# Linear attention with a gated state, then an MLP: one score pair of chunk 3 beside the running sums, and another order of turns

## The chip, the cores and the metric

One core of a Trainium2 chip runs the whole program. The time is device microseconds of one execution; the kernel before has a median of 424.98 us over three runs (424.64 to 425.36). Five engines work beside each other, each in its own program order: TensorE (PE), VectorE (DVE), ScalarE (ACT), GpSimd (POOL), and SyncE (SP), which here only issues DMAs. Semaphores tie them together.

## The reference, cut to what matters

```python
B, H, S, D = 4, 8, 768, 48
for t in range(S):                       # state: [B, H, D, D]
    state = alpha[:, :, t, :, None] * state + einsum('bhd,bhe->bhde', k[:, :, t], v[:, :, t])
    y[:, :, t] = einsum('bhd,bhde->bhe', q[:, :, t], state)
x = y.transpose(0, 2, 1, 3).reshape(B, S, H * D)          # DM = 384
xn = (x - mean) / sqrt(var + 1e-6) * g_ln
out = x + maximum(xn @ w_ch1, 0) @ w_ch2                  # 384 -> 1536 -> 384
```

## The kernel before, in words

The 768 tokens are cut into six chunks (c = 0 to 5) of 128 tokens, and each chunk has four batches b. `attention(c, b)` is one generator for one chunk of one batch; there are 24, named by the letters a to x in the order of `c * 4 + b`, so chunk 3 is m, n, o, p. In a chunk the logarithms of alpha are summed over the tokens by a product with a triangle of ones (the *running sums*, tile `lps`, L310, L313 or L400); from chunk 1 on the sums run over the two halves of 64 tokens apart. ScalarE takes the exponentials (L317, L318), VectorE scales k and q with them (L320, L322, tile `qk`), and both are transposed so that the head dimension lies across partitions: in chunks 0 and 1 by TensorE (L348), from chunk 2 on by VectorE in blocks of 32 x 32 (L359, tile `tr`) and two rounds of DMAs through DRAM: four writes per attention (L365, `td<-tr`) and four reads (L372, into `kT` and `qT`). `tr` lies in a ring of seven buffers (tag `in`) that also holds the raw alpha, k and q.

Then TensorE makes the scores of the four head pairs, 64 x 64 each (L398, tile `aps`); VectorE copies their lower triangle into `at` (L410); the update of the state goes through `ups` (L426), VectorE (L439, tiles `mid` and `st`) and a product with the decay on GpSimd (L441). The outputs `yps` are sums of a product with the state (L457) and one with `at` (L461). ScalarE and VectorE copy them into `x` (L484 and L487), which is also sent to DRAM (L496), normalised, and transposed into `xT` by L520 and L522 or, from chunk 4 on, by L526 and DMAs.

The constant SPLIT decides how the scores of head pair 3 are placed. In a chunk from SPLIT on, they are written into the free columns of the bank that holds the running sums of the attention two further on, with output halves swapped against the other pairs, and their order is alternated with that of pair 2:

```python
split = c >= SPLIT
...
for p, s in () if whole else SCORES if split else np.ndindex(NP, 2):
    for i in range(2):
        rs = slice(64 * i, 64 * i + D)
        to = aps[1][halves[i], 0, s] if split and p == NP - 1 else aps[0][halves[1 - i], p, s]
        nc.tensor.matmul(to, kT[rs, p, s], qT[rs, p, s], start=True, stop=True)
    if ahead:
        ahead.pop(0)()                   # one half of the running sums, two attentions ahead
```

Such a chunk then needs two copies of the triangle (L410, 128 x 384 and 128 x 128) instead of one, two ScalarE copies into `x` (L472, L474) instead of one (L484), two VectorE steps (L477, L480) instead of one (L487), and its swapped half of v is loaded in three DMAs instead of two (L153).

The MLP of chunk 0 is plain: the letters Y and Z make its first product (L556, ReLU in L559), P and Q the second (L568). Chunks 1 to 5 use products of combined blocks, fewer than the plain ones: the letters 1 and 2 make the first products (L846, 15 to a chunk and half, each with its additions on VectorE, L856 to L889, and on GpSimd, L865 to L885), R and U the ReLU (L896), M the second product (L672, additions L682 to L730, L688 on GpSimd). VectorE makes the combined blocks: S and W those of the weights (L798, L632), X those of x (L823), N those of the hidden layer (L659). The letters A to L load the weights as 64-bit floats and turn them into 32-bit floats on VectorE (L215 to L232) and ScalarE (L223). O fetches `kept` copies of x for the sum at the end (L543), and results leave by L547.

All of this is woven together by a literal string, ORDER, with 1508 letters: each letter runs its generator to the next `yield`. The order of each engine's instructions, SyncE's DMAs included, is the order in which these turns issue them; no scheduler moves anything afterwards.

Of the kernel before, what the change touches and what calls it, by code (L numbers as in the profile page):

```python
# [19 lines left out]
STAGED = 3  # L20
BY_DMA = 2
X_BY_DMA = 4
SPLIT = 4
AHEAD = 2
G = 32
SCORES = ((0, 0), (0, 1), (1, 0), (1, 1), (3, 0), (2, 0), (3, 1), (2, 1))
# [4 lines left out]


ORDER = (
    "aaabacdccbbbacbacbadbabbaadababacccbfbeacaAcCdcdacbfdefffeeddedebdaaccaAacacbaab"
    "ffaefeedddefgbCbbcfbhBgcedfcheaggccbcgahhccghdedddgdbidffdhcAcbhfgedfgghAhidjghi"
    "dehCBBZjfigYZYYZZBkYABZjYiCZZhCZffjliijejDYiZeDZjZYDgghfYeZfheekEEgYjgiZYhYZZYZD"
    "legjeEYFYhhfiZiGFhZkGFfgZEZYigikgfjGlYFejfgYHYfkZlkZlfZYfejZHehjYSleiHjGlnfjIjlY"
    "SjHkmInYggmJIYgPSQhJikYQJlPISgKPQgKSliSehSggnKQkhlhelLnSOhLhnkliLOmmmkPkmmhWWOmO"
    "hPPnWSQSohmWXQXlnXoQpPWXpnSlXlPXkQijSjXmXoj21SOjiWookn2o1Xi2om2kS2mXo1k211Wk2222"
    "2S11nmkSnjlimpnplj2ppijJpkrp1m1SW211m1lji1m21212m1linmlnWinURk22pW2q1lr1k2O2jqji"  # L40
    "12i1mn1o1nplnXmUp2pkrrRkrolp1rr2qpU2q11pkRW2Mr2qoM1Uqnk2qlopnMp1RoppoMU1oNLlWNMW"
    "NOosqsRNMNrpm2MNoqtMkkt2lMNM11MonmMrqrqpqtRoXUqMNspttM2MqtNtMsNMNnqNsMMOMtMsMXvX"
    "MMNMMstNsNXqMMOvMnMMrmNXmMuMqMnMnrtruoqpXtrMosX1orMrMvM21q12Xvts1Ot2sr1rMutvXXqu"
    "12211p12u122ru21t1u1222v1O221p221m1Ru2m2U2X22UnqO1v11sxt1w12w2n21usts2Rutpuwsu1K"
    "wU1R2M12vw1qURw1M2NU1or2RMMNMvtMsxtNwooNMsMMM1supvMuvwRNuNwsrUxNNMsMxMNoMrNNMMNt"
    "xMtMMvxxNqMMoMNXMMMMMXMtqMMNqXwvuMMNvxtrMMwXXMM1xMX2OM1tqX1wvstX122221X11rM2u2xu"
    "x1xxwvq221tw2s21xu1w2Xs2ssv1111x2uu1122v22OX212xw11v2r12sUxOR12121wRsUUR112r1xu2"
    "Ux22wNxMsuRU121NRr2N1vMvNNNNMwNMMMMwMNtOuNMXMUMMqXMXMxRXMMNMNwMuvMMMxNM1xMMMXMNN"
    "MXMMNMvMM2MXMXvwuMMMMMXw2X1xw21X1xw2221x11111111112212222OR12O1v222121vwR12U2M2O"
    "2221121211UUR1XR1M222MR11R2XX2XXUM1X2XXOMMNNMN1NUM1XM121NNNNMMU111122M1MN111M1N2"  # L50
    "1MN21MXR2MM21112121X211M1M1MMN1R22M2N2MM22MMRMMO11NM1N2MM1R22UUM2NMMM222222MUMMN"
    "2RMM2MMO2MUNNRUMNNMMOOMMNMMMNNNMMMNMMUMMMNMMMNNMNMMMMMNMMMNMMMMMMMMM"
)


# [1 line left out]
def kernel(  # L57
# [68 lines left out]
    def load(c, m, names):  # L126
# [12 lines left out]
        if "v" in names:  # L139
# [4 lines left out]
            if c:  # L144
# [4 lines left out]
                parts = ((0, 0, NP, NP), (1, 0, NP, 0))  # L149
                if c >= SPLIT:  # L150
                    parts = ((0, 0, NP, NP - 1), (1, 0, NP - 1, 0), (1, NP - 1, 1, H - 1))
# [139 lines left out]
    def attention(c, b):  # L291


        whole, last = c == 0, c + 1 == NCB
        split = c >= SPLIT
        if whole and b % 2 == 0:
# [661 lines left out]
```

## Time and profile before

| what | value |
|---|---|
| median of three runs | 424.98 us |
| the profiled execution, its own time | 425.54 us |
| its span, first to last instruction | 423.8 us |
| mean granted TensorE clock | 0.996 |
| busy: PE, DVE, ACT, POOL | 413.1, 353.8, 179.0, 151.8 us |
| DMA issues by SyncE | 397 |
| DMA, mean | 145 GB/s; 0.9 and more of the 16 engines' time until 90 us, 0.11 in the last 64 us |

The profiled execution took 1.74 us more than its span, and 0.56 us more than the median. A busy engine in this table is one with an instruction in it; the idle time of an engine matters only where the last chain of work runs through it.

### The profile page before, as it was taken

The page shows a single profiled execution, that of the slowest core. Times are in us where ns is not written, and L with a number is a line of the kernel's source. Part 1 is how long each engine was busy: PE and PEld are TensorE (multiplying, and loading weights), DVE is VectorE, ACT ScalarE, POOL GpSimd, SP SyncE. Part 2 cuts the span into 40 slices and gives each one's busy share as a digit, 9 for nine tenths or more (in the row PEclk, how much of TensorE's full clock was granted, in tenths as well). Part 3 has the DMA queues.
Part 4 walks back from the last instruction along what each step waited for, and adds up shares of the span by engine and source line. Part 5 has one row for each costly group of instructions (what it writes and reads, how often), then busy time and mean ns, then how long its engine had stood idle before and what let it go on. Part 6 is the DMA issues. An engine that isn't in the chain of part 4 may idle for free.

```text
span 423.8 us, 11541 instructions
## 1 busy us (share of the span) xinstructions
PE 413.1 (97%) x4608; PEld 364.3 (86%) x4608; DVE 353.8 (83%) x711; ACT 179.0 (42%) x440; POOL 151.8 (36%) x164
## 2 busy tenths in 40 slices
PE   8999999999997999999999999999999999999997
PEld 6887888756686888998888999889998899999996
DVE  3999999999997899895989996679966789757873
ACT  5696447635044566443336612535512333112200
POOL 1010110100022883034395033296051961467314
PEclk9999999999999899999999999999999999999999
DMA  8899989797978678795573345516116200001201
GB/s 279 255 340 265 301 187 296 183 267 184 221 202 176 170 171 177 199 215 132 157 116 115 69 121 129 105 38 180 21 57 140 85 0 2 0 19 39 94 20 56
DMA packets 135037, 61.26 MB, mean 145 GB/s; under 512 B 90908, under 2 KB 131100, under 8 KB 134984
## 3 DMA queue, kind: packets, MB, share of 16 engines
q1 hardware_dynamic: 134440, 60.37, 55.2%
q8 instruction: 36, 0.59, 0.6%
q10 hardware_dynamic: 544, 0.17, 0.2%
q14 instruction: 17, 0.14, 0.1%
HBM read 43.12 MB, written 17.39 MB: 143 GB/s over the span
## 4 chain that ended last, share of the span: by engine, by line
PE 70%; DVE 15%; DMA 8%; issue 3%; SPq 2%; ACT 1%; DVEq 0%; ACTq 0%
PE ops L672 28%; PE hps L846 28%; DMA rq<-in_q_dram 3%; PE hps L556 3%; DVE ws L225 2%; DMA td<-tr 2%; PE aps L398 2%; PE yps L457 2%; DVE w L217 2%; PE yps L461 2%; PE ups L426 1%; DVE tr L359 1%; SPq L365 1%; DVE w L229 1%; DMA gate<-row 1%
## 5 line engine op out<-in xcount | busy, mean ns | idle before, releaser
L688 POOL TENSOR_TENSOR ob<-ob,u 128x192 f32<-128x192 f32 x40 | 28.6, 726 | 57.4 <-DVE ob L685 43.3
L846 PE MATMUL hps<-sum,w 128*128 128x256 f32 x192 | 46.6, 382 | 0.0
L441 POOL TENSOR_TENSOR mid<-mid,gate 112x192 f32<-112x192 f32 x20 | 12.5, 626 | 87.3 <-DVE mid L439 61.9
L896 ACT ACTIVATE hT<-hT 128x512 f32<-128x512 f32 x48 | 28.7, 625 | 32.0 <-POOL hT L868 12.5
L672 PE MATMUL ops<-w,hT 128*128 128x192 f32 x224 | 40.7, 327 | 0.0
L846 PEld LDWEIGHTS hps<-sum,w 128*128 128x128 f32 x192 | 35.8, 190 | 4.9
L672 PEld LDWEIGHTS ops<-w,hT 128*128 128x128 f32 x224 | 37.1, 190 | 0.9 <-ACT hT L896 0.4
L846 PE MATMUL hps<-xT,w 128*128 128x256 f32 x136 | 35.5, 395 | 0.6 <-DVE st L439 0.6
L556 PE MATMUL hps<-xT,w 128*128 128x256 f32 x144 | 32.7, 383 | 0.1
L568 PE MATMUL ops<-w,hT 128*128 128x384 f32 x96 | 31.7, 487 | 0.0
L556 PEld LDWEIGHTS hps<-xT,w 128*128 128x128 f32 x144 | 26.9, 190 | 4.3 <-DVE mid L439 0.5
L846 PEld LDWEIGHTS hps<-xT,w 128*128 128x128 f32 x136 | 26.4, 198 | 4.3 <-DVE st L439 1.0
L672 PE MATMUL ops<-ws,sum 128*128 128x192 f32 x160 | 28.8, 326 | 0.0
L568 PEld LDWEIGHTS ops<-w,hT 128*128 128x128 f32 x96 | 18.0, 190 | 11.8
L672 PEld LDWEIGHTS ops<-ws,sum 128*128 128x128 f32 x160 | 26.6, 190 | 0.2
L682 DVE TENSOR_TENSOR ob<-ops,ob 128x192 f32<-128x192 f32 x50 | 17.3, 350 | 8.5 <-PE ops L672 6.1
L672 PE MATMUL ops<-ws,hT 128*128 128x192 f32 x128 | 23.6, 328 | 0.7 <-DVE hT L887 0.6
L441 POOL TENSOR_TENSOR st<-st,gate 112x192 f32<-112x192 f32 x16 | 9.9, 625 | 37.0 <-DVE st L439 37.0
L398 PEld LDWEIGHTS aps<-qT,kT 48*64 48x64 f32 x576 | 19.4, 134 | 3.9 <-issue 1.4
L672 PEld LDWEIGHTS ops<-ws,hT 128*128 128x128 f32 x128 | 21.3, 190 | 1.8 <-DVE hT L887 1.0
L398 PE MATMUL aps<-qT,kT 48*64 48x64 f32 x576 | 22.4, 222 | 0.2 <-ACT kT L353 0.2
L461 PE MATMUL yps<-vn,at 64*64 64x48 f32 x320 | 22.6, 220 | 0.0
(247 smaller groups left out, 1134.1 us busy)
## 6 DMA issues: line engine op xcount, KB each, us to landing
ws<-in_moe_w_ch_dram SPq DMA_DIRECT2D x12, 768.0 KB
td<-tr SPq DMA_DIRECT2D x64, 96.0 KB
vn<-in_v_dram SPq DMA_DIRECT2D x12, 384.0 KB
kept<-x SPq DMA_DIRECT2D x24, 192.0 KB
ob<-kept SPq DMA_DIRECT2D x24, 192.0 KB
out_dram<-ob SPq DMA_DIRECT2D x19, 192.0 KB
ra<-in_alpha_dram SPq DMA_DIRECT2D x16, 192.0 KB
kT<-td SPq DMA_DIRECT2D x32, 96.0 KB
```

The source lines that it names most:

```text
L217: stt(out=dst, in0=lo.bitcast(UINT32), scalar=2.0 ** -32, in1=dst.bitcast(INT32), op0=AOP.mult, op1=AOP.add)
L225: stt(out=hi, in0=hi, scalar=-(1 << 31), in1=lo, op0=AOP.bitwise_and, op1=AOP.bitwise_or)
L398: nc.tensor.matmul(to, kT[rs, p, s], qT[rs, p, s], start=True, stop=True)
L441: nc.gpsimd.tensor_mul(new, new, by)
L461: nc.tensor.matmul(yps[r][halves[s], i, p], at[halves[r], p, s], by, start=r != i, stop=True)
L556: nc.tensor.matmul(hps, w1[:, j // 2, f, j % 2 * P:][:, :P], xT_of[0][:, f, bs], start=(f == 0), stop=(f == NF - 1))
L568: nc.tensor.matmul(ops_of[b], hT_of[c][:, j, b], w2[:, j], start=(j == 0), stop=(j == NJ - 1))
L672: nc.tensor.matmul(acc, lhs[:, j], rhs[:, j], start=(j == 0), stop=(j == NT - 1))
L682: nc.vector.tensor_add(x, acc, x)
L688: getattr(nc.gpsimd, f"tensor_{op}")(x, x, y)
L846: nc.tensor.matmul(acc[:, i], w, b, start=True, stop=True)
L896: nc.scalar.activation(out=x, in_=x, func=AFT.Relu)
```

## The change

SPLIT goes from 4 to 3: chunk 3 is now treated as chunks 4 and 5 are. For each of m, n, o and p this means one more VectorE copy (L410), one ScalarE copy more, one VectorE step more, and the swapped placing and order of the scores. There are two more DMAs in all (one for each pair of batches of chunk 3): 399. The number of matmuls stays at 2360.

ORDER is another string: the same letters in the same numbers, drawn differently from its first characters on. So nearly every engine's instructions stand in another order.

```diff
-SPLIT = 4
+SPLIT = 3
...
 ORDER = (
-    "aaabacdccbbbacbacbadbabbaadababacccbfbeacaAcCdcdacbfdefffeeddedebdaaccaAacacbaab"
+    "acaaababccdabacbbcadabdacababbeabcbaacccbbcAabddceaafedfceebafdedaedafeccaedegcA"
...
-    "NOosqsRNMNrpm2MNoqtMkkt2lMNM11MonmMrqrqpqtRoXUqMNspttM2MqtNtMsNMNnqNsMMOMtMsMXvX"
+    "pmNMjjoNNNRnMoo2NproNMOksMMkMNtMMkoMNoNMqmnrsqUkNMqpqqsMnrMtttXWMstNvttNMMnMNXoM"
...
-    "2RMM2MMO2MUNNRUMNNMMOOMMNMMMNNNMMMNMMUMMMNMMMNNMNMMMMMNMMMNMMMMMMMMM"
+    "MNMUM12NMMMMRMN2UNMONMNMNMMMNOMMNMMMNMMURNMNMMMMNMMMMMNNMMMMNMMMMMMM"
 )
```

More of the change, by code (lines that the diff above doesn't have):

```diff
@@ L33 @@
 ORDER = (
-    "aaabacdccbbbacbacbadbabbaadababacccbfbeacaAcCdcdacbfdefffeeddedebdaaccaAacacbaab"
[L35 to L39, printed above, removed]
@@ L40 @@
-    "2S11nmkSnjlimpnplj2ppijJpkrp1m1SW211m1lji1m21212m1linmlnWinURk22pW2q1lr1k2O2jqji"
-    "12i1mn1o1nplnXmUp2pkrrRkrolp1rr2qpU2q11pkRW2Mr2qoM1Uqnk2qlopnMp1RoppoMU1oNLlWNMW"
-    "NOosqsRNMNrpm2MNoqtMkkt2lMNM11MonmMrqrqpqtRoXUqMNspttM2MqtNtMsNMNnqNsMMOMtMsMXvX"
-    "MMNMMstNsNXqMMOvMnMMrmNXmMuMqMnMnrtruoqpXtrMosX1orMrMvM21q12Xvts1Ot2sr1rMutvXXqu"
-    "12211p12u122ru21t1u1222v1O221p221m1Ru2m2U2X22UnqO1v11sxt1w12w2n21usts2Rutpuwsu1K"
-    "wU1R2M12vw1qURw1M2NU1or2RMMNMvtMsxtNwooNMsMMM1supvMuvwRNuNwsrUxNNMsMxMNoMrNNMMNt"
@@ L46 @@
[L46 to L51, printed above, removed]
@@ L52 @@
-    "2RMM2MMO2MUNNRUMNNMMOOMMNMMMNNNMMMNMMUMMMNMMMNNMNMMMMMNMMMNMMMMMMMMM"
+    "acaaababccdabacbbcadabdacababbeabcbaacccbbcAabddceaafedfceebafdedaedafeccaedegcA"
+    "bdeadhdCbcfgabbbfdcdggcfgbfbecffeChBccdfeddcgbfhahhfgddgcahdidhgcbeAjgddfhcAhhfi"
+    "BghiYeAjeYefBZjgCiZYeeZYBYgYjZiCZYjZBZlijZfkiYklYZfDjfgDhDYZhCfZgZifYgjZEEYFEgDe"
+    "YgijYYgGgFgYGYYYEZihjFhkfeZkliiZhYGShGZfZjeHkZgYfZFjhiihjeeeHljlHfYlZheYlfelkkIZ"
+    "iZJPYHIQSJgkPhIZnlQSJISPQjKkSfilgKhmgSgKSfgnPjOnLhlmLlgOnknLhmlmOhhmmlmlQhQOikWj"
@@ new lines @@
+    "PmWWhSnWkQlWmnQnpjPSjSkXXiQoXljPXjXoSniSSX1kmlWipml2m1X1SoXS121XokWo21oi1o1222o2"
+    "mnm1m2inWp2im1qpkp2k1in121Xpknp21lplnji12Sn1Wk2222W2kOpmqmXimjU2j2rUn1iS1R1112o2"
+    "1n2m2nrpOp1pRlP1polrrlokR12nrUMrrWrmqjkppq1l1q12p22lolMtkLR21RpMqNMMqoo1UMOpWqUM"
+    "pmNMjjoNNNRnMoo2NproNMOksMMkMNtMMkoMNoNMqmnrsqUkNMqpqqsMnrMtttXWMstNvttNMMnMNXoM"
+    "sMNsX1Mtnm2MXMMqMMpMNMXXmqMsXMMsoMoqnM1XOqM2o22u212Xrrtqtp1mv1q1sq1oXtrv12O211m1"
+    "22r2rrpJv22rstv1r2svts1t1uu2221ru1Rurt221u11r1u12R12tOU2ts1uX22U12Ro22UN21oMM21u"
@@ new lines @@
+    "UvM211ssRMNUp1nqvM1NRvMNMNUxOnMqwNxNNMstMsutupMMMwuNRMMMMwNvuvspvquXsNwvwMxMNwtN"
+    "wXMMrwMtxtMqvXMxNqMMNMMusXvMMMxrMMrXxN2MMXwXXxMrt1xMMMs2X2111svw21M2O1Xt12w22qsK"
+    "s211rt1w221vxwsq1uw22v2212uv2212wuUO111ux212tXxR11111RUxwv2s2q2U21x121R2sM2MsMMU"
+    "v11M2R2RNNNtUrXMMxO11NMMNXuNxxwMvNRMxMXNUNMMMuuMMMNvONNMuMwMNMMMMNXXMNMMMN1XMwMM"
+    "MXMMOuxxMXMwwwMx2vMXw1X21Ou2111122w112x111Xv12121x11w2x1x212112211wu2R212xU11222"
+    "v2121XR12RX212UMO22212UR2XNXXMRXXXMX2ONUUMMMN1MM1211N22N1M1XN1R2MM121M2X121MMN1M"
@@ L53 @@
+    "11N1U2R1MN1112211MN1M11NRM21NNMMMM2R21MM222122MNMOURMM222UM1NMN2M222M2MOMMU22MMM"
+    "MNMUM12NMMMMRMN2UNMONMNMNMMMNOMMNMMMNMMURNMNMMMMNMMMMMNNMMMMNMMMMMMM"
 )
```

## The prediction

> **What bounds the kernel now.** I read the page's busy times first, then a table of stretches, then PE's waits, and then the instructions around the longest wait.
>
> ```profile
> span 423.8 us, 11541 instructions
> PE 413.1 (97%) x4608; PEld 364.3 (86%) x4608; DVE 353.8 (83%) x711; ACT 179.0 (42%) x440; POOL 151.8 (36%) x164
> ```
>
> PE is busy for all but 10.7 us of the span. The number of matmuls does not change, so at most those 10.7 us, what a slow clock costs, and what the scores gain can be won. PE's waits in order of size:
>
> ```profile
> PE hps L846 <- DVE hT L858: 1.9, 1, 1.9
> PE lps L250 <- DVE more L247: 1.1, 1, 1.1
> PE hps L846 <- ACT hT L876: 0.7, 1, 0.7
> PE tps L348 <- DVE qk L322: 0.7, 1, 0.7
> PE xps L520 <- ACT x L484: 0.6, 1, 0.6
> PE ops L672 <- DVE hT L887: 0.6, 1, 0.6
> PE hps L846 <- DVE st L439: 0.6, 1, 0.6
> ```
>
> The first and the last of these stand at 133 and 136 us, 1.87 and 0.60 us by the timeline. The table of stretches (busy time of PE, PEld, DVE, ACT, POOL, then the granted clock) shows what follows them:
>
> ```profile
> 90.00:120.00 30.00, 30.00 (x384) 20.32 (x383) 29.53 (x55) 10.50 (x24) 1.39 (x2) 1.00 0.89 213
> ...
> 132.00:142.00 10.00, 7.54 (x114) 5.49 (x113) 7.06 (x13) 4.10 (x12) 3.99 (x5) 0.83 0.79 184
> ...
> 136.00:138.00 2.00, 1.40 (x4) 1.18 (x4) 2.00 (x5) 1.93 (x6) 0.77 (x1) 0.66 1.08 190
> 138.00:140.00 2.00, 2.00 (x6) 1.35 (x4) 1.04 (x2) 0.63 (x4) 1.41 (x3) 0.50 0.90 202
> ```
>
> From 132 to 142 us PE idles 2.46 us, and the clock of 0.83 costs another 0.17 x 10 = 1.7 us: 4.2 us in one place, the largest loss of the program. Before it, DVE has no gap to speak of (29.53 of 30). The cause is in DVE's timeline and SyncE's (the bracket is idle time and what ended it):
>
> ```profile
> 121.53 0.97 DVE L359 STREAM_TRANSPOSE tr<-qk 128x768 f32<-128x768 f32 x1
> ...
> 130.01 0.55 DVE L322 TENSOR_TENSOR qk<-rq,eq 128x384 f32<-128x384 f32 x1
> 133.27 0.98 DVE L359 STREAM_TRANSPOSE tr<-qk 128x768 f32<-128x768 f32 x1 [2.71 <-DMA td<-tr]
> 134.18 0.65 DVE L858 TENSOR_TENSOR hT<-hps,hT 128x512 f32<-128x512 f32 x1
> ```
>
> and, on SyncE's side:
>
> ```profile
> 126.65 2.78 SPq L365 DMA_DIRECT2D td<-tr  x4
> ```
>
> The seventh transposition ends at 122.5; SyncE, busy with loads, gets to its four `td` writes only at 126.65; the eighth takes a buffer that those writes must have left and stands 2.71 us at the head of DVE's queue. The L858 behind it, which would free a bank for PE, is late with it.
>
> **How I weigh the new order.** For each engine I add up the start-to-start times of its instructions in program order, by form, from the rows (L359 0.90, L858 and its like 0.60, L410 0.62, L846 0.432 per matmul). Up to 121 us real time is DVE's sum + 10.9 and PE's sum + 7.9, nearly constant from 95 us on. I call *lead* PE's sum before an instruction minus DVE's sum through the one that it needs; PE waits where the lead is under 10.9 - 7.9 = 3.0 plus what DVE has idled since. This gives back the wait above: the lead of L858 is 3.78, DVE's idle 2.7, so 5.7 - 3.78 = 1.9, as measured.
>
> **The change part by part.**
>
> *The wait at 133 us.* In the new order the seventh transposition ends 2.9 us later in DVE's sum (114.4 against 111.5), so at 125.4, and its `td` writes are the 157th to 160th issues instead of the 158th to 161st. SyncE reached them at 126.65 without waiting for the transposition, so one issue fewer (0.5 us) makes 126.1, the last at 128.9, and landed 3.9 us later as before (129.4 to 133.3): 132.8. The eighth is ready at 131.4, since only 6.0 us of DVE work stand between the two instead of 8.1. DVE's idle: 1.4 us instead of 2.7. What PE needs after it is drawn later: the smallest leads are 4.15 and 4.17, against 3.78 and 2.91 before. So PE waits 3.0 + 1.4 - 4.15 = 0.25, I take 0.3, and the clock stays up: -4.2 + 0.3 = **-3.9**. Bounds: 0 (DVE does not idle) to 3.0 + 2.7 - 4.15 = 1.5 us, or 3.2 with a slow clock behind it.
>
> On the clock, rows say that 1.87 and 0.60 us of idle within 4 us of time brought it to 0.50 for over 2 us. The Trainium skill ("TensorE: Matmul & The Clock Gate", HAM oscillation) has the clock fall only behind idle gaps of over some 3.4 us; by that rule no wait here would cost more than itself, and this term would be -2.2 instead of -3.9. The trace differs, and the measured clock decides.
>
> *Three short waits*, at 161.8, 196.3 and 229.1 us (0.63, 0.68, 0.63, together 1.9): in the first two no PE work stands between the matmul that fills a bank and the one that needs ACT to have emptied it. In the new order the like happens once (an L672 behind the L472 copy, with 0.14 us of PE work for a copy of 0.34 and some 0.25 of hand-over: 0.45), nearly so a second time (0.1), and twice an L887 or L878 has 1.19 us for its 0.60 (together 0.4): 1.0. **-0.9**; bounds 0 and -1.9.
>
> *The scores.* Timeline of a chunk without the split, and of chunk 4 with it, from the first record to the start of what follows:
>
> ```profile
> 94.83 0.27 PE L398 MATMUL aps<-qT,kT 48*64 48x64 f32 x2
> ...
> 95.91 0.33 PE L520 MATMUL xps<-consts,xn 128*128 128x128 f32 x1
> ```
> ```profile
> 198.88 0.27 PE L398 MATMUL aps<-qT,kT 48*64 48x64 f32 x2
> ...
> 199.59 0.24 PE L398 MATMUL lps<-qT,kT 48*64 48x64 f32 x2
> ...
> 199.78 0.36 PE L426 MATMUL ups<-vn,qk 64*48 64x48 f32 x11
> ```
>
> That is 1.08 us against 0.90, running sums included; where other small products stand beside them the gain is nearer 0.05. I take 0.1 for each of four: **-0.4**; bounds 0 and -0.7. The Trainium skill ("TensorEngine Tiling (Array Packing)", Gotcha 1: PSUM Pressure) says that different row tiles cannot use one bank at the same time, and the split puts scores and running sums of both row tiles into one; by it this term would be 0. In the rows above they run beside each other.
>
> *The added work.* Per attention DVE gets L410 in 0.49 + 0.19 for 0.62 and L477 + L480 in 0.64 for 0.48, together 0.22, so 0.9 us for four; ACT 0.04; SyncE two issues (0.5 to 0.7 each). The leads above count DVE's part already. ACT is half idle.
>
> *Tight places elsewhere.* Before 121 us the smallest leads are 2.93 (at PE's sum 67, where 2.6 are needed), 3.28 and 3.07 (at 109 and 119, where 3.0 are needed), against 1.95 and 3.14 before: no wait if DVE idles no more than it did. It may: between the fifth and sixth transposition stand 6.3 us of DVE work for 6.6 before, and a decay column (L416) and two weight loads are needed 0.5 to 1 us sooner after their issue. No row shows what slack these had; each idle us of DVE here goes to PE in full. **+0.7**, bounds 0 and +2.0. What hides the rest is the later `kT` and `qT` reads: from the end of each transposition to its scores the new order leaves as much or more in nearly every pair (16.8 for 15.0, 18.4 for 17.2, 15.4 for 14.5 in the three tightest of chunk 3). The start before 45 us and the last 3 us behind PE hold the same steps; I put them at 0, +-0.5.
>
> Sum: -3.9 - 0.9 - 0.4 + 0.7 = -4.5. On the profiled execution's own time that is 425.54 - 4.5 = 421.0 (span 419.3), and 0.56 less at the median's level: **420.5 us**.
>
> **The rivals.**
>
> *The wait moves rather than goes* (0.20). DVE idles 2.7 as before, PE waits 1.5, and the clock falls behind it (1.7): the place still costs 3.2. For it: the eighth transposition follows the seventh more closely. Against: the writes no longer wait long behind loads. 425.0 - 1.0 - 0.9 - 0.4 + 0.7 = 423.4.
>
> *The early part loses* (0.17). DVE idles 2 us more before 119 us, at the weights, the decay columns and the sixth transposition: 2.0 for 0.7, so 421.8; with the start's 0.5, 422.3.
>
> *SyncE is as late behind the transpositions as it was* (0.10). If landing again takes 10.8 us from the end of the seventh (122.5 to 133.3), it comes at 136.2, DVE idles 4.8, PE waits 3.0 + 4.8 - 4.15 = 3.6, and 1.7 for the clock: 5.3 for 4.2, +1.1. The fifth and sixth, tighter too, then lose 1.0, and the short waits return (0). 425.0 + 1.1 + 1.0 - 0.4 = 426.7: slower. It turns from a gain to a loss where the landing takes 9.7 us. Against it: those 10.8 us were mostly a queue that the new order meets 2.9 us nearer its end.
>
> *Chunk 3's scores gain nothing*: 420.9, inside the forecast.
>
> **How the numbers follow.** The forecast has 0.48; better still, with all early waits gone, 0.05: 419.0 to 419.8. With the bounds of -0.3 for the first wait, -1.0 for the short ones, -0.7 for the early ones and -0.5 for the start the low end is 418.0. The high end is the first rival with the 1.3 us more of the early part: 424.7. Beyond it lie the slower rival and part of "no change". 0.2% is 0.85 us, about what a measurement of this kernel can tell from no change. Faster: the forecast, the better case, and both gentle rivals, less what of these could land within 0.85 us of before: 0.84. Same 0.06. Slower 0.10.
>
> **What would show it.** Right: no PE wait over 1 us behind 10 us; clock 1.00 in every slice; DVE's idle before the eighth L359 at 0 to 2 us; PE's idle at 6 to 7 us in place of 10.7; chunk 3's scores at 0.9 to 1.0 us. Wrong: a wait of over 2 us on DVE between 110 and 190 us with a clock under 0.9 behind it, or PE's offset at 110 us above 9 us.

## The result, and the profile after

The changed kernel has a median of 422.24 us over ten runs (421.73 to 422.84). Ten runs of the kernel before have 425.45 us (424.64 to 430.29). The medians differ by 3.2 us. The ratio is 0.9911, with a 95% interval of 0.9884 to 0.9938: faster by 0.9%. The forecast was 4.5 us and a time of 420.5 us; the measured time lies inside its range and 1.7 us above its centre. The profiled execution took 422.69 us. From its profile:

```profile
span 420.9 us, 11590 instructions
PE 412.4 (98%) x4608; PEld 363.4 (86%) x4608; DVE 353.9 (84%) x723; ACT 179.5 (43%) x444; POOL 152.2 (36%) x164
```

TensorE's waits, the longest first (engine, line, what it waited for; then us in all, how often, the longest):

```profile
PE tps L348 <- DVE qk L322: 1.2, 1, 1.2
PE lps L250 <- DVE more L247: 1.1, 1, 1.1
PE tps L348 <- ACT qT L355: 1.0, 1, 1.0
PE lps L310 <- ACT la L305: 0.7, 1, 0.7
PE ops L672 <- ACT x L472: 0.5, 1, 0.5
PE lps L400 <- DVE ob L572: 0.2, 1, 0.2
```

The first four lie before 40 us, in the start. Behind it the longest is 0.5 us; the 1.9 on L858 and the 0.6 on L439 of the kernel before are gone. The stretches that were shown of before, now after:

```profile
90.00:120.00 30.00, 29.95 (x442) 20.20 (x441) 29.53 (x55) 11.35 (x27) 3.68 (x5) 1.00 0.86 210
132.00:142.00 10.00, 9.75 (x191) 8.30 (x183) 9.78 (x18) 4.07 (x12) 8.50 (x7) 1.00 0.83 210
136.00:138.00 2.00, 2.00 (x59) 1.56 (x59) 1.90 (x4) 0.00 (x0) 1.60 (x1) 1.00 0.49 80
138.00:140.00 2.00, 1.97 (x33) 1.57 (x25) 1.91 (x5) 1.45 (x6) 2.00 (x2) 1.00 0.78 257
```

PE is busy for 9.75 of the ten microseconds that had 7.54, and the granted clock (the figure behind the brackets) stays at 1.00. VectorE's timeline and SyncE's show why:

```profile
123.92 0.97 DVE L359 STREAM_TRANSPOSE tr<-qk 128x768 f32<-128x768 f32 x1
...
129.93 0.55 DVE L322 TENSOR_TENSOR qk<-rq,eq 128x384 f32<-128x384 f32 x1
...
131.40 0.97 DVE L359 STREAM_TRANSPOSE tr<-qk 128x768 f32<-128x768 f32 x1
132.30 0.65 DVE L864 TENSOR_TENSOR u<-u,hps 128x512 f32<-128x512 f32 x1
```
```profile
125.43 2.66 SPq L365 DMA_DIRECT2D td<-tr  x4
```

The `td` writes follow their transposition by 0.5 us instead of 4.2, and the eighth transposition carries no wait in brackets: it begins the moment VectorE is free.

**Where PE's time went.** I added up PE's start-to-start times in the traces by four kinds: the start (up to the first large product, L556), the large products (L556, L568, L672, L846), the small ones between them (scores, running sums, states, outputs, transpositions), and waits over 0.06 us. "Cuts" is how many times a stretch of small products interrupts the large ones. All in us; the last product's own 0.3 us is in no column, and the last four rows are described below.

| profile | start | large | small | cuts | waits | PE's last end |
|---|---|---|---|---|---|---|
| before | 38.36 | 328.45 | 49.00 | 26 | 4.61 | 420.75 |
| after | 37.71 | 327.00 | 51.49 | 33 | 1.35 | 417.87 |
| before, second profile | 39.14 | 326.77 | 49.67 | 26 | 8.88 | 424.78 |
| before, third profile | 38.54 | 326.55 | 49.04 | 26 | 5.33 | 419.80 |
| after, second profile | 37.80 | 327.03 | 51.35 | 33 | 1.94 | 418.44 |
| new order, SPLIT 4 | 37.48 | 326.80 | 50.30 | 33 | 1.15 | 416.06 |

From the first row to the second: start -0.65, large products -1.45 (mostly the clock), waits -3.26, small products +2.49, together -2.87. The waits fell by 3.26 us where the forecast has 2.4 (the clock left out). The small products are where the forecast went wrong.

### The profile page after: what moved, and what is told of

It is laid out like the page before. It is cut to its first block, busy times and chain, and to the rows that moved or that the text cites. A ratio compares the mean times of both kernels' runs of the same rounds, so it can differ in the third digit from the quotient of the medians.

```text
span 420.9 us, 11590 instructions
## 1 busy us (share of the span) xinstructions
PE 412.4 (98%) x4608; PEld 363.4 (86%) x4608; DVE 353.9 (84%) x723; ACT 179.5 (43%) x444; POOL 152.2 (36%) x164
## 4 chain that ended last, share of the span: by engine, by line
PE 80%; DVE 14%; DMA 2%; issue 2%; SPq 0%; POOL 0%; ACT 0%; DVEq 0%; POOLq 0%
PE ops L672 31%; PE hps L846 29%; PE ops L568 7%; PE aps L398 2%; PE yps L457 2%; PE ups L426 2%; PE yps L461 2%; DVE w L229 2%; DVE w L217 2%; DMA rq<-in_q_dram 1%; DVE ws L225 1%; PE tps L348 1%; DVE at L410 1%; PE hps L556 1%; PE xps L520 1%
## 5 line engine op out<-in xcount | busy, mean ns | idle before, releaser
L688 POOL TENSOR_TENSOR ob<-ob,u 128x192 f32<-128x192 f32 x40 | 27.0, 686 | 66.6 <-DVE ob L685 56.6
L846 PE MATMUL hps<-sum,w 128*128 128x256 f32 x192 | 47.4, 383 | 0.2 <-issue 0.2
L672 PE MATMUL ops<-w,hT 128*128 128x192 f32 x224 | 41.2, 328 | 0.5 <-ACT x L472 0.5
L846 PEld LDWEIGHTS hps<-sum,w 128*128 128x128 f32 x192 | 35.9, 190 | 5.5 <-issue 0.5
L672 PEld LDWEIGHTS ops<-w,hT 128*128 128x128 f32 x224 | 37.1, 190 | 1.7 <-ACT x L472 0.6
L846 PE MATMUL hps<-xT,w 128*128 128x256 f32 x136 | 34.1, 381 | 0.2 <-ACT x L484 0.2
L556 PE MATMUL hps<-xT,w 128*128 128x256 f32 x144 | 32.8, 383 | 0.1
L568 PE MATMUL ops<-w,hT 128*128 128x384 f32 x96 | 32.0, 488 | 0.0
L556 PEld LDWEIGHTS hps<-xT,w 128*128 128x128 f32 x144 | 26.8, 190 | 3.9 <-DVE mid L439 0.2
L672 PE MATMUL ops<-ws,sum 128*128 128x192 f32 x160 | 28.6, 326 | 0.0
L846 PEld LDWEIGHTS hps<-xT,w 128*128 128x128 f32 x136 | 25.3, 190 | 3.6 <-ACT x L484 0.3
L568 PEld LDWEIGHTS ops<-w,hT 128*128 128x128 f32 x96 | 17.9, 190 | 11.6
L672 PEld LDWEIGHTS ops<-ws,sum 128*128 128x128 f32 x160 | 26.5, 190 | 0.2
L672 PE MATMUL ops<-ws,hT 128*128 128x192 f32 x128 | 23.6, 328 | 0.0
L461 PE MATMUL yps<-vx,at 64*64 64x48 f32 x320 | 23.1, 220 | 0.1
L457 PEld LDWEIGHTS yps<-st,qT 48*64 48x64 f32 x320 | 19.6, 134 | 4.0 <-issue 2.3
L457 PE MATMUL yps<-mid,qT 48*64 48x48 f32 x320 | 22.1, 222 | 0.0
```

Source lines behind the costliest of these rows:

```text
L457: nc.tensor.matmul(yps[i][halves[s], i, p], qT[rs, p, s], (now, mid)[s][rs, p], start=True, stop=r != i)
L461: nc.tensor.matmul(yps[r][halves[s], i, p], at[halves[r], p, s], by, start=r != i, stop=True)
L556: nc.tensor.matmul(hps, w1[:, j // 2, f, j % 2 * P:][:, :P], xT_of[0][:, f, bs], start=(f == 0), stop=(f == NF - 1))
L568: nc.tensor.matmul(ops_of[b], hT_of[c][:, j, b], w2[:, j], start=(j == 0), stop=(j == NJ - 1))
L672: nc.tensor.matmul(acc, lhs[:, j], rhs[:, j], start=(j == 0), stop=(j == NT - 1))
L688: getattr(nc.gpsimd, f"tensor_{op}")(x, x, y)
```

## The experiments

Kernels measured together ran on one chip, beside runs of the kernel before. Three such groups, on three chips, gave the kernel before medians of 427.60, 427.46 and 426.55 us, so ratios hold only within a group. Where a run's mean clock is quoted, it is the one recorded with that run.

**The order alone, and the split alone.** First the new ORDER with the old SPLIT, then the old ORDER with the new SPLIT.

```diff
-SPLIT = 3
+SPLIT = 4      # in the kernel after: only the order is new
```

> The new order alone: SPLIT stays at 4. If the gain is the drawn order, above all the wait at 133 us that is gone, it stays whole: 421.9 to 422.9 us against 425.2, and the scores of chunk 3 cost 0 to 0.4 more. If the split carries the gain, this lies within 0.8 us of the kernel before. Third reading: the split costs more on VectorE (the first statistics step of chunk 3 took 1.12 us once instead of 0.26, beside a GpSimd addition) than it gains on PE; then this is faster than the change itself, by 0.3 to 0.8 us.

Measured: 421.77 us (420.76 to 421.98), 0.9863 of before (0.9832 to 0.9894).

```diff
-SPLIT = 4
+SPLIT = 3      # in the kernel before: only the split is new
```

> SPLIT = 3 with the order of before. If the order is the gain: within 0.8 us of the kernel before (424.4 to 426.0), the eighth L359 waiting 2.7 us or up to 0.6 more for the td writes (one more vx issue stands ahead of them). If the split were the gain: 422 to 423.

Measured: 428.92 us (426.89 to 432.79), 1.0044 of before (1.0010 to 1.0078). The order carries the whole gain. The split of chunk 3 brings nothing by itself; by the interval this kernel is even 0.1 to 0.8% slower, which was not expected. Its small products stand at 49.36 us, against 49.00 to 49.67 in three profiles without the split, so in this profile it is not they that make it slower; its waits add up to 6.81 us, 1.51 of them at a place that comes back below.

**One turn moved.** In the kernel before, the transposition that waits is moved behind the VectorE turns L858, L798 and L632; nothing else changes.

```diff
-"...2ppijJpkrp1m1SW211m1lj..."
+"...2ppijJkr1m1SWp2p11m1lj..."
```

> The kernel before with two letters moved: the eighth transposition stands behind three VectorE steps (L858, L798, L632, together 2.07 us) instead of ahead of them; SyncE's queue and all else as before. If the loss at 133 us is VectorE's queue held by one instruction that waits for the td writes: the wait of L359 falls from 2.7 to about 0.6 us, PE waits 0 to 0.8 us there instead of 2.5, the clock stays at 1.00, and the time falls by 3 to 4 us to 421.3 to 422.3. If PE is held by the sum of VectorE's work and not by this wait, the idle time comes back within the next 50 us and the time falls by under 1 us.

Measured: 426.74 us (424.35 to 430.28), 0.9996 of before (0.9964 to 1.0028). The wait for `td` is gone and PE is busy for all of 132 to 142 us, at a clock of 1.00. Yet no time was won. In its trace two others stand instead, in PE's timeline (time, duration, instruction, then the idle time before it and what ended it):

```profile
131.73 0.25 PE L457 MATMUL yps<-mid,qT 48*64 48x48 f32 x1 [1.80 <-issue]
...
184.81 1.41 PE L672 MATMUL ops<-ws,hT 128*128 128x192 f32 x7 [1.48 <-DVE hT L659]
```

The second goes back to a load: VectorE's L685 waited for `ob<-kept` (shown below). The first is ended by no semaphore ("issue"). The DMA traffic from 122 to 129 us, by queue (packets, MB, share), first of the kernel before, then of this one:

```profile
q1 hardware_dynamic: 3342, 1.19, 69.4%
q8 instruction: 1, 0.02, 1.2%
```
```profile
q1 hardware_dynamic: 3167, 1.62, 84.9%
```

The 16 KB of instructions that came at 122.4 us are missing here. They came at 129.08, took 1.07 us, and PE went on 1.58 us after that. The split-alone kernel had the same: a load from 128.47 to 129.35, and PE standing 1.51 us until 130.99, 1.64 us after the load. Is it this order, or chance? The same kernel again, for a second profile:

> The kernel before with only one transposition turn moved behind three VectorE turns, unchanged, for a second profile. In its first profile the wait in front of the eighth transposition was gone, but PE stood 1.80 us at 129.9 with no semaphore to end it, and an instruction load that begins at 122.4 us in the profile of the kernel before began only at 129.08 and ended 1.6 us before PE went on; a further 1.5 us went at 184.6 (L672 behind the L659). Theory: the instruction load is late by chance, so it is a matter of the execution and not of this order: this profile has the load at 122 to 124 us and no gap at 130, or, if it is late again, the gap again with it, of the same 1.5 to 1.6 us behind the load's end. Rival: the gap at 130 is a wait on VectorE (L322 ended 0.05 us before PE went on); then the gap is there whatever the time of the load, and ends with L322.

Measured (428.04 us): the load at 126.54, which is 1.5 us behind the start of the seventh transposition (0.9 in the kernel before, 6.4 in the first profile of this one), and no such gap. It lost 0.82 us at the place of the old wait (137.6 us), 0.52 at the L672, and 1.03 and 0.83 in front of scores (152 and 63 us). So the gap comes by chance and not by this order. In the twelve profiles without extra writes, four waits behind 40 us are ended by no semaphore: these two, and one at 197 us in each profile of the kernel after (0.22 and 0.66 us). Each ends 1.4 to 1.6 us behind the end of a 16 KB load. That PE stood for want of instructions is read from this; no run puts a load late on purpose, and what makes one late stays open.

**The loads out of SyncE's way.** In the kernel before, the three loads of the next alpha, k and q are issued behind the four `td` writes instead of ahead.

```diff
+        if later == 4 * B:
+            pass
-        if c < 2 and b % 2:
+        elif c < 2 and b % 2:
...
                     td writes of attention o
+            if later == 4 * B:
+                load_one(later)
```

> The kernel before with the loads of alpha, k and q of the 17th attention issued behind the td writes of the seventh transposition instead of ahead of them. If those writes are late because SyncE's queue is, three issues fewer bring them 1.5 us forward (first at 125.1 instead of 126.65): L359 waits about 1.0 us instead of 2.7, PE 0 to 1 us, the clock stays up, and the time falls by 2.5 to 4 us. If the landing and not the issue sets it (a full memory path), the first issue comes forward, but the wait stays over 2 us and the time within 0.8 us of before.

Measured: 426.26 us (423.04 to 430.12), 0.9969 of before (0.9937 to 1.0001). The profiled execution is the shortest of its runs (423.04 us). In it the mechanism of the prediction is plain (lines are shifted by 2 to 4):

```profile
124.93 2.29 SPq L367 DMA_DIRECT2D td<-tr  x4
```
```profile
130.87 0.98 DVE L361 STREAM_TRANSPOSE tr<-qk 128x768 f32<-128x768 f32 x1
```

The writes go out 1.7 us sooner, the transposition does not wait, and PE has 9.82 of 10 us from 132 to 142. But the L672 behind `ob<-kept` now waits 0.92 us instead of 0.09, and the runs of this kernel scatter over 7.1 us, those of the kernel before beside them over 4.7.

**What the old order does from run to run.** Two more profiles of the kernel before, unchanged.

> The kernel before, unchanged, for a second profile. Its times scattered from 424.6 to 430.3 us so far, those of the new order from 420.8 to 422.8. Theory A: the old order has places where PE hangs on an event whose time varies from run to run, and the first profile caught one of the shorter runs. Then this profile, if it is of a longer run, shows the extra microseconds in one or two PE gaps behind 120 us: at the eighth transposition (133 us, 1.87 us in the first profile, now 3 to 5), or in front of the L457 products at 130 us, where the profile of the kernel with only one turn moved has 1.8 us of PE idle that no semaphore ends and an instruction load 7 us later than in the first profile. Rival B: the old order is slower everywhere by a little (clock or DMA load of this chip); then all stretches are longer by the same share and no gap grows by more than 0.5 us.

> The kernel before, unchanged, for a third profile. The first lost 2.5 us of PE time between 132 and 142 us and 1.7 to the clock there; the second lost 1.7 there with no fall of the clock, and 4.1 more on loads and reads that had not landed (L426 at 70.8, 104.1; L398 at 152.7). Theory: the order has several places where PE hangs on a DMA's landing by less than the scatter of landings, so a third profile has again 1.5 to 3 us at the eighth transposition, and 0 to 4 us on landings at places that need not be the same. Rival: two fixed states, one like the first profile and one like the second; then it repeats one of the two within 0.3 us at each place.

Measured: 429.56 and 424.58 us. The waits of the longer one:

```profile
PE ups L426 <- DMA vn<-in_v_dram: 2.5, 3, 1.7
PE aps L398 <- DMA qT<-td: 1.2, 1, 1.2
PE hps L846 <- DVE hT L858: 1.1, 1, 1.1
PE ops L672 <- DVE hT L659: 1.1, 1, 1.1
```

and the stretch of the eighth transposition in it, then in the third profile:

```profile
132.00:142.00 10.00, 8.31 (x172) 6.61 (x166) 8.06 (x15) 5.48 (x18) 3.39 (x4) 1.00 0.84 170
```
```profile
132.00:142.00 10.00, 7.81 (x123) 6.13 (x122) 8.19 (x15) 5.39 (x14) 5.07 (x6) 1.00 0.86 196
```

The wait at the eighth transposition is there in all three profiles (1.87, 1.09, 1.59 us, each with 0.60 behind it), but its fall of the clock only in the first. The rest of the scatter is landings. VectorE's L685, which needs `ob<-kept`, in the kernel before, its second profile and the one with a turn moved:

```profile
181.78 0.62 DVE L685 TENSOR_TENSOR ob<-ob,ops 128x192 f32<-128x192 f32 x2 [0.24 <-DMA ob<-kept]
```
```profile
185.81 0.62 DVE L685 TENSOR_TENSOR ob<-ob,ops 128x192 f32<-128x192 f32 x2 [1.45 <-DMA ob<-kept]
```
```profile
181.94 0.62 DVE L685 TENSOR_TENSOR ob<-ob,ops 128x192 f32<-128x192 f32 x2 [2.06 <-DMA ob<-kept]
```

Each idle time there costs PE about 0.15 to 0.6 us less than itself (0.09, 1.06 and 1.48 us). That the executions are of two fixed kinds is ruled out: the third profile has 0.76 us of waiting for a load of v at 68 us, where the first had none and the second 1.68 at 71. Of 29 runs of the kernel before in the first group, 11 had a mean clock of 0.995 or 0.996 and a median of 428.2 us, 18 had 0.999 or 1.0 and 426.95. In the first profile the clock was at 0.50 from 136.7 to 140.1 us; one such stretch makes a mean of 0.996 over 424 us (an estimate: half of 3.4 us is 0.4% of the span).

**The kernel after again, and the stretched step.** An unchanged second profile of the kernel after; and the kernel after with L477 as an instruction that reads one SBUF operand instead of two.

> The kernel after, unchanged, beside the next two so that they can be compared on one chip, and for a second profile. 421.7 to 422.8 us expected. If the old order's scatter comes from variable waits that the new order keeps off PE's path, then this profile agrees with the first one of the kernel after within 0.5 us at every stage; if the new order also has such a place, some gap of PE differs by over 1 us between the two profiles.

```diff
-stt(out=yps[1][:, :, m], in0=xv[:, :, m], scalar=-1.0 / DM,
-    in1=zero_col..., op0=AOP.mult, op1=AOP.add, accum_out=off)
+nc.vector.tensor_scalar(out=yps[1][:, :, m], in0=xv[:, :, m], scalar1=-1.0 / DM,
+                        scalar2=0.0, op0=AOP.mult, op1=AOP.add, accum_out=off)
```

> The kernel after, with the L477 step as a tensor_scalar (times -1/384, plus 0.0, with the sum) instead of a scalar_tensor_tensor with a second SBUF operand of zeros. Same result, same number of instructions. In the profile of the kernel after, L477 took 1.12 us once at 145.4, beside a GpSimd product from 145.10 to 146.37, for a median of 0.26. Theory: VectorE instructions that read two SBUF operands stretch to the end of a GpSimd tensor product beside them. Then no L477 takes over 0.5 us here, L823 and L659, which still read two, still have instances at twice their median or more, and the time falls by 0.2 to 0.6 us, since VectorE is behind PE at 146 to 161 us. Rival: the stretch has to do with the accumulating read behind L477 or with any VectorE instruction beside GpSimd; then L477 still has an instance of about 1 us, and the time is unchanged (within 0.2 us).

The kernel after again: 422.88 us (421.96 to 423.22), 0.9897 of before (0.9875 to 0.9918). Its stages repeat the first profile's within 0.2 us but for one gap, the wait for instructions at 197 us: 0.66 us for 0.22. GpSimd and VectorE in the first profile of the kernel after, twice:

```profile
139.83 1.26 POOL L871 TENSOR_TENSOR hT<-u 128x512 f32<-128x512 f32 x1
139.90 1.48 DVE L823 TENSOR_TENSOR sum<-sum,xT 128x256 f32<-128x256 f32 x1
```
```profile
145.10 1.27 POOL L872 TENSOR_TENSOR hT<-hT 128x512 f32<-128x512 f32 x1
```
```profile
145.38 1.12 DVE L477 SCALAR_TENSOR_TENSOR yps<-x,small 128x96 f32<-128x96 f32 x1
```

L823 takes 0.42 us in the median and L477 0.26. Both stretch to shortly behind the end of the GpSimd product beside them. In this profile three of the twelve L477 begin beside a GpSimd product; they take 1.12, 0.53 and 0.96 us, and the other nine 0.26. It is not the kind of instruction: L480 and L487 are the same operation with one of its two operands in PSUM, and none of the eight that begin beside a GpSimd product takes longer than the others, this one for example beside a product that ends at 139.86:

```profile
139.25 0.55 DVE L487 SCALAR_TENSOR_TENSOR x<-yps,x 128x384 f32<-128x384 f32 x1
```

With L477 on one operand:

```profile
144.91 1.28 POOL L871 TENSOR_TENSOR hT<-hT 128x512 f32<-128x512 f32 x1
```
```profile
145.18 0.25 DVE L477 TENSOR_SCALAR_CACHE_REDUCE yps<-x 128x96 f32<-128x96 f32 x1
```
```profile
139.71 1.48 DVE L822 TENSOR_TENSOR sum<-sum,xT 128x256 f32<-128x256 f32 x1
```

L477 no longer stretches (none of the twelve over 0.26); L823, which still reads two, does, once even for 2.20 us (at 275.8), where PE loses nothing by it. The wait of 0.23 us in front of L400 at 148.8 is gone, the small products fall from 51.35 to 50.85 us, and PE ends at 416.40 instead of 418.44; 0.9 of these 2.0 us are waits, 0.5 small products. Counted from the same large product at 145 us to the same one at 152, PE takes 6.02 us instead of 6.89, in both profiles of the kernel after: 0.87 us, 0.64 of it in small products and 0.23 in that wait. The two other stretched L477 cost PE nothing. In the medians this is 422.07 us (421.17 to 424.38) against 422.88, which the scatter does not separate. The Trainium skill ("SBUF — State Buffer", Who interferes with whom) says that a VectorE instruction with two SBUF inputs and a GpSimd instruction that reads SBUF exclude each other, and that the later one waits for the end of the other. The trace agrees; the prediction passed over this page, although the change adds four such L477.

**Both mended.** The new order, SPLIT 4, and L477 with one operand.

> New order, chunk 3 without the split (SPLIT 4), and the tensor_scalar at L477 in chunks 4 and 5. The new order with SPLIT 4 had 421.77 us on another occasion, the kernel after 422.24. Theory: the split of chunk 3 costs 0.5 us in the new order, and the two-operand stretch at most 0.2 where chunk 3 has no L477: 421.3 to 421.8, that is 0.3 to 0.9 under the kernel after in this same call. Rival: the 0.5 us between the two was a difference of the occasions; then this kernel and the one after agree within 0.2 us.

Measured: 422.10 us (421.40 to 423.01), 0.9884 of before (0.9860 to 0.9907): the same as with the split and the mended L477. With L477 mended, small products take 50.83 us without the split in chunk 3 and 50.85 with it. That they agree is chance: between 40 and 100 us, ahead of chunk 3, this profile has 0.4 us of small products that the four others of the new order do not have. Behind 100 us the split still takes 0.4 us more of them (38.9 for 38.4), 0.3 of it between 162 and 180 us, and 0.1 less of waits. So what the split cost in the new order was the stretched L477 and some 0.4 us more, for which no run shows the cause. The new order with SPLIT 4 (421.77 us) has the lowest median of all, but no interval separates it from these two.

**SyncE late on purpose.** Eight small extra writes, 128 x 2 numbers each, issued ahead of the `td` writes of attention o, once in the kernel after and once in the kernel before.

```diff
+            if c * B + b == 14:
+                for i in range(8):
+                    pad = dram.tile([P, 2], FP32, name="pad", tag="pad", bufs=8)
+                    nc.sync.dma_start(pad, g_col[:, :2])
```

> The kernel after, with eight small extra DMA writes (128 x 2 into a scratch tensor that nobody reads) issued by SyncE ahead of the four td writes of attention o, the seventh to be transposed. Each takes SyncE 0.4 to 0.5 us, so those td writes start at some 128.3 us instead of 125.0 and land at some 134.8 instead of 131.4. In both profiles of the kernel after VectorE reaches the eighth transposition at 131.4 without waiting. Theory: how late SyncE is here is what made the wait of the kernel before; then the bracket of a wait on td<-tr is back in front of the eighth L359, 3 to 3.8 us, PE idles 2.0 to 2.9 us on an L846 behind 133 us, and the time is 2 to 4.5 us above the kernel after (424.2 to 427.0 us, the upper end if the clock falls too). Rival: the reserve in the new order (6 us of other VectorE work and a lead of PE's supply of over 4 us) swallows it: under 1 us more.

> The kernel before with the same eight extra DMA writes in the same place, ahead of the four td writes of attention o. There SyncE comes to these writes late already (126.7 us for a transposition that ended at 122.5), so each extra issue should be added to VectorE's wait in full: 2.7 + 3.6 = 6.3 us in front of the eighth L359, PE idle 1.9 + 3.6 = 5.5 us, and 3 to 5 us more than the kernel before in this call. Rival: the wait ends with something other than SyncE's queue, or the microseconds come back at the places behind it that waited before (152, 187, 197 us): under 2 us more.

Measured: 435.86 us in the new order, 1.0231 of before (1.0197 to 1.0266), and 440.03 us in the old, 1.0334 (1.0287 to 1.0381). That is about 13 us more in each, three times what was expected. New order, SyncE, then VectorE, PE, and two stretches (lines shifted by 4):

```profile
125.53 6.23 SPq L367 DMA_DIRECT2D pad<-small  x8
132.35 5.17 SPq L369 DMA_DIRECT2D td<-tr  x4
```
```profile
144.28 0.98 DVE L359 STREAM_TRANSPOSE tr<-qk 128x768 f32<-128x768 f32 x1 [12.00 <-DMA td<-tr]
```
```profile
145.89 1.65 PE L850 MATMUL hps<-sum,extra 128*128 128x256 f32 x3 [9.52 <-DVE u L868]
```
```profile
130.00:140.00 10.00, 5.71 (x113) 4.24 (x111) 2.29 (x6) 3.98 (x11) 2.14 (x2) 1.00 0.80 27
140.00:150.00 10.00, 4.11 (x10) 3.31 (x11) 5.61 (x11) 0.00 (x0) 3.58 (x3) 0.55 0.81 142
```

and the old order's transposition:

```profile
147.48 0.98 DVE L359 STREAM_TRANSPOSE tr<-qk 128x768 f32<-128x768 f32 x1 [15.12 <-DMA td<-tr]
```

The mechanism holds: late `td` writes bring the wait back in the new order. The dose was wrong. Eight kilobytes in 1024 packets of 8 bytes took SyncE 0.78 us an issue and held the DMA engines at 0.80 busy for 27 GB/s; the `td` writes behind them took 5.17 us to issue and had landed 6.8 us later still. What the pair does measure is the reserve: of VectorE's idle time PE is spared 12.00 - 9.52 = 2.5 us in the new order, and 15.12 - 13.80 = 1.3 us in the old.

## Why the prediction was right or wrong

*The wait at 133 us* (-3.9): right, as a wait and as a size against the profile that it was read from. 2.46 us of idle and 1.7 of clock became 0.25 us and none. That the 0.25 is the forecast's own figure is luck: 0.21 of it is a wait for ScalarE's copy (L484, at 133.6 us), not for VectorE. The eighth transposition was forecast to idle 1.4 us and idled 0: SyncE began the writes at 125.43 instead of 126.1, and they had landed by 131.4, at most 3.3 us after the last issue, where I had taken 3.9. That the issue queue was the cause of this wait is shown from both sides, by the loads moved and by the extra writes. What I could not see in one profile: the 1.7 us of clock were in one execution of three.

*Three short waits* (-0.9): 0.63, 0.68 and 0.63 became 0.51 and 0.07: -1.35. A wait for instructions of 0.22, which I had not foreseen, takes some of it back.

*Early and new tight places* (+0.7): too high. Behind 40 us and outside the places above, waits were 0.22 us before and 0.33 after: +0.1. The start, set at 0, gave -0.65.

*The scores* (-0.4): this is the step that failed, in size and sign. From the first record of each score stretch to the start of what follows, as the prediction measured, chunk 3's four stretches take 4.03 us in the kernel before and 3.81 with the split in the old order. In the new order they take 4.29 without the split, 4.80 with it, 0.23 of which is a wait, and 4.34 with the split and L477 on one operand. So the split gained 0.2 us in the old order and nothing in the new one. The unsplit stretch of 1.08 us that I compared was among the longer ones: chunk 3 of the kernel before has 1.10, 1.05, 0.94 and 0.94. And what a split stretch needs stands behind it: one more VectorE step with two SBUF operands. I added 0.9 us of VectorE work to the leads and did not ask what runs on GpSimd beside it. L477 stood 0.86 us longer at 145.4, and PE lost 0.87 us by 152, all of which comes back when L477 reads one operand. In PE's sum of small products the split made +1.2 (51.49 for 50.30, the new order without it): 0.6 of that is the stretched L477, and the rest stays open. Whether the rule on one bank for different row tiles has a part in that rest is not settled by any run.

*A term that was missing.* Without the split in chunk 3 the new order's small products still take 50.30 to 50.83 us, against 49.00 to 49.99 in seven profiles of the old order. The new order cuts the large products 33 times instead of 26, so each of the seven further cuts goes with some 0.16 us (1.1 us between the means). I had weighed the order by leads only, with a price per instruction that does not depend on its neighbours. No run changes the cuts alone, so that the cuts cause it is argued, not shown.

The sum: -4.5 forecast. Small products came out 2.9 higher; the start, the tight places and the short waits, with the 0.22, 1.5 lower; the large products 0.25 higher than the clock alone makes them. That gives -2.87, as PE's ends show.

*The rivals.* The wait did not move, the early part did not lose, SyncE was not as late. "Chunk 3's scores gain nothing" came true and was sized too low, since it had no price for a loss. What no rival had is that the time of before is itself a draw: my base, 424.98 us, comes from three of its shorter runs. Beside the kernel after in one group it was 427.46 against 422.88, a gain of 4.6 us.

*What would show it.* No clock below 1.00 and no idle before the eighth L359: right. PE's idle at 6 to 7 us of the span: wrong, 420.9 - 412.4 = 8.5. No wait over 1 us behind 10 us: missed by 1.03 us on L348 at 32.9. Chunk 3's scores at 0.9 to 1.0 us: right for one of the four (0.91, 1.14, 1.08, and 1.67 with its wait).

*The clock.* It fell behind gaps of 1.87 and 0.60 us in the first profile, and stayed at 0.50 for 3.4 us; it did not fall behind 1.59 and 0.60, or 1.09 and 0.60. With the extra writes it was at 0.50 for 10.2 us in the new order (from 140.9 us) and for 17.1 in the old (from 137.4): three and five times the first. The Trainium skill ("TensorE: Matmul & The Clock Gate", Part 1) calls the activity window free-running and has the slow start of the same kernel differ from run to run for it. The traces agree in so far as the fall came in one execution of three. The first profile still contradicts the rule of 3.4 us of idle, which the prediction names.

## What to carry to other kernels

Read more than one profile before pricing a wait that ends with a DMA: here the same place cost 4.2, 1.7 and 2.2 us in three executions, and a kernel whose waits behind the start sum to 1.1 to 2 us in every profile is worth more than one that removes the longest wait of one trace. Taking one such wait out of the old order, by a turn or by a queue, bought nothing that could be measured. In the first profile of each VectorE's L685 stood longer for `ob<-kept` instead (2.06 and 1.37 us for 0.24), so PE may only have come sooner to the next landing; no run tests that by itself. And when a step is added on VectorE, count its SBUF operands and look at what GpSimd does beside it.

## What the runs showed of the hardware

- A VectorE instruction of 0.26 us with two SBUF operands took 0.53 to 1.12 us where it began beside a GpSimd product, one with a single SBUF operand in the same places 0.25, and the same operation with one of its two operands in PSUM kept its time there.
- TensorE stood 1.8 and 1.5 us, with no semaphore to wait for, when a 16 KB load of instructions began 6.4 and 6.2 us behind the seventh transposition instead of 0.9 to 1.6, and went on 1.6 us after the load's end, both times.
- 1024 DMA packets of 8 bytes, 8 KB in all, took 6.2 and 6.5 us to issue and delayed the transfer behind them in the queue by some 12 us: it was waited for until 18.6 and 23.2 us behind its transposition's end, and without them until 6.5 at most and 10.8.
- The clock was at 0.50 for 3.4, 10.2 and 17.1 us in three executions: one, three and five times 3.4.
- None of 32 runs of the four kernels in the new order without extra writes had a mean clock under 0.999; of 51 runs of the kernel before in the three groups, 18 had.
